# Top-k attention and an MLP on one core: two units' scores in one group, paired hidden tiles, and five pairs of units transposed on TensorE

## The chip, the core and the metric

The kernel runs on one core of a Trainium2 chip. The time is device microseconds of one execution. Of five runs of the kernel before, the median is 1507.03 us (1506.27 to 1509.31). The profile is of the execution that took 1509.31 us. Engines are named as in the profile: PE (TensorE matmul), PEld (its weight loads), DVE (VectorE), ACT (ScalarE), POOL (GpSimd) and SP (SyncE, which here issues all DMAs).

## What is computed

```
scores = q k^T / sqrt(64)                  8 batches x 8 heads, 576 x 576, from 64 channels
kth    = 32nd largest of each row
attn   = softmax(where(scores >= kth, scores, -1e9))
x      = (attn @ v), heads side by side:   4608 tokens x 512
h      = x @ w_in                          512 -> 2048
out    = max(0.01 h, h) @ w_out            2048 -> 512
```

All inputs are 32-bit floats except the two weights, which arrive as 64-bit floats.

## The kernel before

**Rounding.** The weights come in 16 pieces of 64-bit words. `round_weights` turns each into 32-bit floats in three parts: ACT and POOL take the words apart; DVE makes scale and mantissa, and six matmuls with scaled identities add the parts up in PSUM; DVE multiplies by the scale (L147). The loop at L429 runs the parts of three pieces staggered. At its step 15 the scores of units 0 and 1 are issued, ahead of piece 15's second part.

**Units.** Attention is cut into 144 units of 128 rows. A whole unit is 128 queries of both heads of a pair; a left unit is the 64 queries that remain, of two pairs. A unit's score tile `s_sb` is 128 x 2 x 576. Its life, one line per stage:

- `scores` (L191): q k^T into two PSUM tiles `psc0` and `psc1`, two banks each, one for each head, in halves of 288 keys; then two ACT copies to `s_sb` (L207). Two heads use the two halves of the array's rows.
- `top_k` (L209): DVE finds the 32 largest of each row, in four rounds of MAX8 and MATCH_REPLACE8.
- `mask` (L228): POOL, two operations for each head. `exponents` and `sums` (L237, L241): ACT.
- `reciprocals` (DVE, L245), `normalize` (ACT, L249).
- `transpose` (L252): ACT splits each 32-bit word into two 16-bit halves (L259), SP stores them to DRAM, and one transposing DMA brings them back as `wT`.
- `weigh_values` (L276): 20 matmuls with v into the PSUM tile `po`, which two units share; `keep_values` (L290): ACT copies to `x`.

**MLP.** Tokens go in 19 chunks, two of 128 and seventeen of 256. `mlp` (L323) is a generator that yields after every few matmuls. For each of 16 blocks f of the hidden layer it has four matmuls into a PSUM tile `ph` and one Prelu to the tile `gT[f]` (L339); then 2 x 16 matmuls into `pz` (L345), a copy (L352) and a store. The first two chunks use `hidden_of_few` (L301), with the operands exchanged and TensorE transposes (L318). `ph`, `pz` and `pt` share three banks (pool `ps_ml`). PSUM has eight banks: four for `psc`, one for `po`, three for `ps_ml`.

**Order.** Every engine runs its instructions in the order in which the loop at L445 issues them; nothing is reordered. In step s, unit s is in `top_k`, unit s-1 in mask and exponents, unit s-2 in reciprocals, normalize and transpose. In even steps the scores of units s+2 and s+3 are issued, with the values of two units between them. `values_at` (L384) says at which step a unit's values are taken:

```
def values_at(n):
    return n + LAG + (n + LAG) % 2        # LAG = 3
```

The MLP fills in between, seven times a step, by `mlp_steps`. `slot_budget` divides a chunk's remaining cost evenly over the slots until the next chunk is ready. A chunk is ready when its last unit's values are: chunk 0 (units 0 to 3) in step 6, chunk 1 (4 to 7) in step 10, chunk c (units 8c-8 to 8c-1, for c from 2) in step 8c+2. So PE's order in an even step is MLP, scores, values, scores, MLP.

Of the kernel before, what the change touches and what calls it, by code (L numbers as in the profile page):

```python
# [19 lines left out]
def kernel(  # L20
# [25 lines left out]
    HS = S // 2  # L46
    NFC = DFF // P
# [16 lines left out]
    ps_po = ctx.enter_context(tc.tile_pool(name="ps_po", bufs=1, space=bass.MemoryType.PSUM))  # L64
    ps_ml = ctx.enter_context(tc.tile_pool(name="ps_ml", bufs=3, space=bass.MemoryType.PSUM))
# [10 lines left out]
    gT = [const.tile([P, CHMAX], F32, name=f"gT{f}") for f in range(NFC)]  # L76
# [26 lines left out]
    def round_weights(n):  # L103
# [22 lines left out]
        if n + 1 < NPIECE:  # L126
            nc.scalar.activation(scale, scale, AF.Copy, bias=-896.0 * 128, scale=128.0)
        else:
            nc.vector.tensor_scalar(scale, scale, 896.0, 128.0, ALU.subtract, ALU.mult)
        nc.vector.tensor_scalar(m_top, top, 0xF, 0x3F80, ALU.bitwise_and, ALU.bitwise_or)  # L130
        nc.vector.tensor_scalar(top, top, 0x8000, None, ALU.bitwise_and)
        if n < NPIECE - 3:
            pw = ps_sc.tile([P, 2, 512], F32, name=f"psc{n % 2}")
            sums = [(pw[:, h, :], h * 512) for h in range(2)]
            ends = [(pw.rearrange("p h n -> p (h n)"), 0)]
        else:
            ends = sums = [(ps_ml.tile([P, 512], F32, name="pw", tag="ml"), h * 512) for h in range(2)]
# [53 lines left out]
    def scores(u):  # L191
        ps = [ps_sc.tile([P, 2, 512], F32, name=f"psc{i}") for i in range(2)]
        for n in range(0, len(u.parts), 2):
            for half in range(2):
                for i, pi, side, r0 in u.parts[n:n + 2]:
                    qt, kt = qk_of[pi]
                    d = slice(side * D, (side + 1) * D)
                    nc.tensor.matmul(  # L198
                        ps[i][r0:r0 + u.rows, half, 0:HS],
                        qt[d, u.q0:u.q0 + u.rows],  # L200
                        kt[d, half * HS:(half + 1) * HS],
                        start=True, stop=True,
                    )
        u.both = work.tile([P, 2, S], F32, name="s_sb", bufs=5)
        u.s = [u.both[:, i, :] for i in range(2)]
        for i in range(2):
            nc.scalar.copy(u.s[i].rearrange("p (h n) -> p h n", h=2), ps[i][:, :, 0:HS])  # L207

# [54 lines left out]


# [36 lines left out]
    def hidden_of_few(x):  # L301

        g_of = {}
        for j in range(NFC // 4 + 1):
            if j < NFC // 4:
                ph = ps_ml.tile([P, 512], F32, name="ph", tag="ml")
                for c in range(HP):
                    nc.tensor.matmul(ph, x[c][:, 0:P], w_in[c][:, j * 512:(j + 1) * 512],  # L308
                                     start=(c == 0), stop=(c == HP - 1))
                    if c == 1:  # L310
                        yield 2 * 512
                g_of[j] = raws.tile([P, 2 * DMODEL], U16, name="scale", bufs=2).bitcast(F32)
                nc.scalar.activation(g_of[j], ph, AF.Prelu, alpha=SLOPE)
                yield 2 * 512
            if j:
                pt = ps_ml.tile([P, 4, P], F32, name="pt", tag="ml")
                for i in range(4):
                    nc.tensor.transpose(pt[:, i, :], g_of[j - 1][:, i * P:(i + 1) * P], ident)  # L318
                for i in range(4):
                    nc.scalar.copy(gT[4 * (j - 1) + i][:, 0:P], pt[:, i, :])  # L320
                yield 2 * P

    def mlp(ch):  # L323
# [6 lines left out]
        for f in range(NFC if ch >= EARLY else 0):  # L330
            ph = ps_ml.tile([P, 512], F32, name="ph", tag="ml")
            for c in range(HP):
                nc.tensor.matmul(  # L333
                    ph[:, 0:n], w_in[c][:, f * P:(f + 1) * P], x[c][:, 0:n],
                    start=(c == 0), stop=(c == HP - 1),
                )
                if c == 1:
                    yield 2 * max(n, 225)
            nc.scalar.activation(gT[f][:, 0:n], ph[:, 0:n], AF.Prelu, alpha=SLOPE)  # L339
            yield 2 * max(n, 225)  # L340
        for r0 in range(0, n, P):
            m = min(P, n - r0)
            pz = ps_ml.tile([P, 512], F32, name="pz", tag="ml")
            for f in range(NFC):
                nc.tensor.matmul(  # L345
                    pz[0:m, 0:DMODEL], gT[f][:, r0:r0 + m], w_out[f // 4][:, f % 4, :],
# [35 lines left out]
    LAG = 3  # L382

    def values_at(n):  # L384

        return n + LAG + (n + LAG) % 2
# [29 lines left out]
    with tc.manual_schedule():  # L416
# [12 lines left out]
        for n in range(NPIECE + 2):  # L429
# [8 lines left out]
            elif n == NPIECE - 1:  # L438
                for u in steps[0:2]:
                    scores(u)  # L440
            if n == NPIECE - 1:
                load_v(0)
                load_v(1)

        for s in range(len(steps) + LAG + 1):  # L445
# [8 lines left out]

            slot()
# [3 lines left out]
            mlp_steps(budget)  # L459
            slot()  # L460
# [7 lines left out]
            if older:  # L468
# [9 lines left out]
            for u in new[:1]:  # L478
                scores(u)
            if s % 2 == 0:  # L480
                po = ps_po.tile([P, 2, P], F32, name="po")
                for values in (weigh_values, keep_values):
                    for n, u in enumerate((unit(s - LAG - 1), unit(s - LAG))):
                        if u:
                            values(u, po[:, n, :])
                attended(s)
            for u in new[1:]:
                scores(u)
# [63 lines left out]
```

## Time and profile before

| | |
|---|---|
| median of 5 runs | 1507.03 us |
| profiled execution, time and span | 1509.31 us, 1507.5 us |
| PE busy | 1427.1 us, 95% |
| PEld, DVE busy | 933.6, 1328.1 us (62%, 88%) |
| ACT, POOL busy | 1111.5, 1097.6 us (74%, 73%) |
| mean granted PE clock | 0.973 |
| ACT idle before L207 / L339, waiting for PE | 112.9 / 94.4 us |
| DVE idle before `rz` (L247), waiting for ACT | 74.2 us |
| PE waiting for `wT` (L283) | 26.0 us, 9 times |
| PE waiting for L207's evictions | 27.0 us, 9 times, the longest 22.0 |

Busy is time in which an engine works on something; an engine that is busy all the time sets the pace only if the chain of waits that ends last runs through it. The page cuts the span into 40 slices of about 37.7 us and gives each engine's busy share in tenths; PEclk is the clock that TensorE was granted, in tenths of full speed. A group line of the page gives the line, the engine, the operation with output and inputs, the count, then busy time, mean length of one, and the idle time before them with what ended it. Matmuls are pipelined: a record's length contains its way through the array, so the pace is read from the starts. A 32-bit matmul shows as two records.

### The profile page before, as it was taken

How to read it: one execution, taken by the hardware profiler on the slowest of the kernel's cores; microseconds unless marked ns; L12 is line 12 of the kernel's file. 1: busy time of each engine (PE TensorE's matmuls, PEld its weight loads, DVE VectorE, ACT ScalarE, POOL GpSimd, SP SyncE). 2: the span in 40 equal slices, each digit the busy share in tenths (PEclk: the TensorE clock that was granted, in tenths of full speed). 3: DMA queues.
4: the chain of work that ended last, by engine and by line, in shares of the span. 5: the costliest groups of instructions: out<-in, count | busy, mean ns of one | idle time of the engine just before them, and what ended most of it. 6: DMA issues, size and time to landing. Idle time of an engine off the chain costs nothing.

```text
span 1507.5 us, 24130 instructions
## 1 busy us (share of the span) xinstructions
PE 1427.1 (95%) x8030; PEld 933.6 (62%) x8032; DVE 1328.1 (88%) x3414; ACT 1111.5 (74%) x2140; POOL 1097.6 (73%) x742
## 2 busy tenths in 40 slices
PE   6727987999999999999999999999999999999998
PEld 2314445666666766666766666766666666666774
DVE  7898999999999999899999998999999989999600
ACT  8646887878787877787878777878777777777720
POOL 2278788878788877787888787878887877788600
PEclk9956998999999999999999999999999999999999
DMA  8623465645655556655665455645655565655510
GB/s 323 244 63 111 133 169 164 173 129 152 180 156 151 137 154 169 158 139 148 181 170 142 132 166 159 174 127 151 188 163 141 127 170 144 149 144 139 138 51 14
DMA packets 399294, 227.03 MB, mean 151 GB/s; under 512 B 343360, under 2 KB 343361, under 8 KB 397121
## 3 DMA queue, kind: packets, MB, share of 16 engines
q1 hardware_dynamic: 399168, 225.49, 53.8%
q8 instruction: 63, 1.03, 0.3%
q14 instruction: 63, 0.51, 0.1%
HBM read 46.14 MB, written 94.37 MB: 93 GB/s over the span
## 4 chain that ended last, share of the span: by engine, by line
PE 84%; DVE 11%; DMA 3%; ACT 1%; issue 1%; POOL 0%; DVEq 0%; ACTq 0%; SPq 0%
PE pz L345 31%; PE ph L333 31%; PE psc L198 10%; PE po L283 10%; DVE tops L221 4%; DVE pairs L224 3%; DMA wT<-apart 2%; PE ph L308 1%; DVE pairs L216 1%; DVE w_in L147 1%; DVE scale L144 1%; DVE w_out L147 1%; DMA apart<-split 0%; ACT split L259 0%; DVE scale L123 0%
## 5 line engine op out<-in xcount | busy, mean ns | idle before, releaser
L234 POOL TENSOR_SCALAR pen<-s_sb,tops 128x576 f32<-128x576 f32 x288 | 638.4, 2217 | 237.8 <-DVE tops L221 205.7
L221 DVE MAX8 tops<-pairs 128x8 f32<-128x288 f32 (+1 forms) x1152 | 635.6, 591 | 0.0
L345 PE MATMUL pz<-w_out,gT 128*128 128x512 f32 x1152 | 506.7, 595 | 0.0
L333 PE MATMUL ph<-x,w_in 128*128 128x256 f32 x2176 | 483.0, 381 | 0.0
L224 DVE MATCH_REPLACE8 pairs<-tops,pairs 128x288 f32<-128x288 f32 (+1 forms) x864 | 459.9, 537 | 0.0
L333 PEld LDWEIGHTS ph<-x,w_in 128*128 128x128 f32 x2176 | 409.3, 190 | 77.6 <-issue 20.2
L235 POOL TENSOR_TENSOR s_sb<-s_sb,pen 128x576 f32<-128x576 f32 x288 | 406.8, 1412 | 24.0
L345 PEld LDWEIGHTS pz<-w_out,gT 128*128 128x128 f32 x1152 | 215.9, 190 | 264.5 <-issue 263.6
L259 ACT COPY split<-s_sb 128x1152 uint16<-128x1152 uint16 x288 | 315.6, 1144 | 0.0
L207 ACT COPY s_sb<-psc 128x576 f32<-128x576 f32 x288 | 169.3, 639 | 112.9 <-PE psc L198 112.9
L250 ACT ACTIVATE s_sb<-s_sb,rz 128x576 f32<-128x576 f32 x288 | 206.7, 767 | 32.2 <-DVE rz L247 32.2
L238 ACT ACTIVATE s_sb<-s_sb,nbias 128x576 f32<-128x576 f32 x288 | 221.4, 769 | 11.1 <-POOL s_sb L235 11.1
L198 PE MATMUL psc<-kt,qt 64*128 64x288 f32 (+1 forms) x1280 | 198.5, 442 | 27.1 <-ACT s_sb L207 27.0
L216 DVE TENSOR_TENSOR pairs<-s_sb 128x576 f32<-128x576 f32 x288 | 213.6, 780 | 9.9
L283 PE MATMUL po<-wT,vt 128*64 128x128 f32 (+1 forms) x3200 | 182.5, 270 | 26.2 <-DMA wT<-apart 26.0
L283 PEld LDWEIGHTS po<-wT,vt 128*64 128x64 f32 x3200 | 162.7, 140 | 58.5 <-DMA wT<-apart 30.1
L198 PEld LDWEIGHTS psc<-kt,qt 64*128 64x128 f32 (+1 forms) x1280 | 111.2, 182 | 99.4 <-ACT s_sb L207 36.6
L339 ACT ACTIVATE gT<-ph 128x256 f32<-128x256 f32 x272 | 99.0, 380 | 94.8 <-PE ph L333 94.4
L247 DVE RECIPROCAL rz<-ze 128x2 f32<-128x2 f32 x144 | 22.4, 155 | 74.8 <-ACT ze L243 74.2
L297 ACT COPY x<-po 128x128 f32<-128x128 f32 (+1 forms) x160 | 32.5, 263 | 62.8 <-PE po L283 62.6
L224 DVE MATCH_VALUE_LOAD pairs<-tops,pairs 128x8 f32 x864 | 62.1, 72 | 0.0
L352 ACT COPY o_sb<-pz 128x512 f32<-128x512 f32 x36 | 21.1, 586 | 53.9 <-PE pz L345 53.9
(44 smaller groups left out, 391.8 us busy)
## 6 DMA issues: line engine op xcount, KB each, us to landing
apart<-split SPq DMA_DIRECT2D x288, 288.0 KB, 2.1
raw<-in_weights_dram SPq DMA_DIRECT2D x16, 1024.0 KB, 6.4
vt<-in_vk_dram SPq DMA_DIRECT2D x32, 320.0 KB, 3.7
qt<-in_qT_dram SPq DMA_DIRECT2D x32, 288.0 KB, 3.6
kt<-in_kT_dram SPq DMA_DIRECT2D x32, 288.0 KB, 4.0
out_dram<-o_sb SPq DMA_DIRECT2D x36, 256.0 KB, 2.0
wT<-apart SPq DMA_TRANSPOSE x144, 4.6
```

What stands on the lines that cost most here:

```text
L198: nc.tensor.matmul(ps[i][r0:r0 + u.rows, half, 0:HS], qt[d, u.q0:u.q0 + u.rows], kt[d, half * HS:(half + 1) * HS], start=True, stop=True,)
L216: nc.vector.tensor_tensor(pairs[:, :, n, :], u.both[:, :, 0:HS], u.both[:, :, HS:S], op)
L221: nc.vector.max(out=u.tops[:, i, r, :], in_=rest[i])
L224: nc.vector.match_replace(out=rest[i], in_to_replace=u.tops[:, i, r, :], in_values=rest[i], imm_value=LOWEST)
L234: nc.gpsimd.tensor_scalar(pen, u.s[i], u.tops[:, i, ROUNDS - 1, 7:8], MASKED, ALU.is_lt, ALU.mult)
L235: nc.gpsimd.tensor_tensor(u.s[i], u.s[i], pen, ALU.add)
L238: nc.scalar.activation(u.s[i], u.s[i], AF.Exp, bias=u.nbias[:, i:i + 1], scale=SCALE, accum_out=u.z[:, i:i + 1])
L250: nc.scalar.activation(u.s[i], u.s[i], AF.Copy, bias=0.0, scale=u.rz[:, i:i + 1])
L259: nc.scalar.copy(split, pairs[:, :, h])
L283: nc.tensor.matmul(po[side * D:(side + 1) * D, o, :], vt[:, c, side, :], u.wT[:, c + side * NKC if c + 1 < NKC else c, r:r + n], start=(c ...
L333: nc.tensor.matmul(ph[:, 0:n], w_in[c][:, f * P:(f + 1) * P], x[c][:, 0:n], start=(c == 0), stop=(c == HP - 1),)
L345: nc.tensor.matmul(pz[0:m, 0:DMODEL], gT[f][:, r0:r0 + m], w_out[f // 4][:, f % 4, :], start=(f == 0), stop=(f == NFC - 1),)
```

## The change

**Scores.** `scores` takes both units of a step. Their 576 columns are cut in 352 (WIDE) and 224 (NARROW) instead of 288 and 288. Each unit has a wide tile of two banks (tag "wide", two buffers); both units' narrow parts share one tile of two banks ("narrow"). The matmuls are issued as u0 wide, u0 narrow, u1 narrow, u1 wide, then four ACT copies in that order. `po` has no bank of its own any more and is a "wide" tile too. Until step 20 the scores come before the values, from then on after them.

**MLP.** `ps_ml` has two banks. A `ph` tile holds two blocks f, with one Prelu for both; `gT` is one tile with a dimension for f.

**Hurried pairs.** The pairs of units (2,3), (6,7), (14,15), (22,23) and (30,31), the last of chunks 0 to 4, have their values one step earlier. They are transposed by nine TensorE transposes and two ACT copies. The second unit of a pair is normalized and transposed at the very start of its step, ahead of the top-k.

**Rounding.** Unit 0's scores are issued after piece 12's matmuls, unit 1's after piece 15's. Piece 14's scale moves from ACT to DVE, and pieces use other PSUM tiles.

```diff
-    ps_po = ctx.enter_context(tc.tile_pool(name="ps_po", bufs=1, space=bass.MemoryType.PSUM))
-    ps_ml = ctx.enter_context(tc.tile_pool(name="ps_ml", bufs=3, space=bass.MemoryType.PSUM))
+    ps_ml = ctx.enter_context(tc.tile_pool(name="ps_ml", bufs=2, space=bass.MemoryType.PSUM))
...
-        if n + 1 < NPIECE:
+        if n < NPIECE - 2:
             nc.scalar.activation(scale, scale, AF.Copy, bias=-896.0 * 128, scale=128.0)
...
-        if n < NPIECE - 3:
-            pw = ps_sc.tile([P, 2, 512], F32, name=f"psc{n % 2}")
+        if n < NPIECE - 4 or n % 2 == 0:
+            tag, bufs = ("wide", 2) if n < NPIECE - 4 else ("narrow", 1)
+            pw = ps_sc.tile([P, 2, 512], F32, name=tag, bufs=bufs)
...
+    def scores(us):
+        narrow = ps_sc.tile([P, 2, 512], F32, name="narrow")
+        ps = {}
+        for k, u in enumerate(us):
+            wide = ps_sc.tile([P, 2, 512], F32, name="wide", bufs=2)
+            ps[u] = ((wide[:, :, 0:WIDE], 0, WIDE),
+                     (narrow[:, :, k * NARROW:(k + 1) * NARROW], WIDE, S))
+
+        order = ((us[0], 0), (us[0], 1), (us[1], 1), (us[1], 0))
+        for u, part in order:
+            to, k0, k1 = ps[u][part]
+            for n in range(0, len(u.parts), 2):
                 for i, pi, side, r0 in u.parts[n:n + 2]:
...
+                    nc.tensor.matmul(to[r0:r0 + u.rows, i, :], qt[d, u.q0:u.q0 + u.rows],
+                                     kt[d, k0:k1], start=True, stop=True)
+        for u in us:
+            u.both = work.tile([P, 2, S], F32, name="s_sb", bufs=5)
+            u.s = [u.both[:, i, :] for i in range(2)]
+        for u, part in order:
+            to, k0, k1 = ps[u][part]
+            nc.scalar.copy(u.both[:, :, k0:k1], to)
...
+    def transpose_in_haste(u):
+
+        u.wT = work.tile([P, 2 * NKC - 1, P], F32, name="wT", bufs=3)
+        both = u.both.rearrange("p i n -> p (i n)")
+        for c0, c1 in ((0, 8), (8, 2 * NKC - 1)):
+            pt = ps_sc.tile([P, 2, 512], F32, name="wide", bufs=2)
+            pt = pt.rearrange("p h (c n) -> p (h c) n", n=P)
+            for c in range(c0, c1):
+                nc.tensor.transpose(pt[:, c - c0, :], both[:, c * P:(c + 1) * P], ident)
+            nc.scalar.copy(u.wT[:, c0:c1, :], pt[:, 0:c1 - c0, :])
...
+        for f0 in range(0, NFC if ch >= EARLY else 0, 2):
+            ph = ps_ml.tile([P, 2, CHMAX], F32, name="ph", tag="ml")
+            for i in range(2):
+                f = f0 + i
+                for c in range(HP):
+                    nc.tensor.matmul(
+                        ph[:, i, 0:n], w_in[c][:, f * P:(f + 1) * P], x[c][:, 0:n],
+                        start=(c == 0), stop=(c == HP - 1),
+                    )
+                    if c == 1 or i == 0 and c == HP - 1:
+                        yield 2 * max(n, 225)
+            nc.scalar.activation(gT[:, f0:f0 + 2, 0:n], ph[:, :, 0:n], AF.Prelu, alpha=SLOPE)
...
+    HURRY = 20
+    HURRIED = {3, 7, 15, 23, 31}
 
     def values_at(n):
 
-        return n + LAG + (n + LAG) % 2
+        return n + LAG + (n + LAG) % 2 - ((n | 1) in HURRIED)
...
-            elif n == NPIECE - 1:
-                for u in steps[0:2]:
-                    scores(u)
+            elif n == NPIECE - 3:
+                first_scores(steps[0])
+            elif n == NPIECE:
+                first_scores(steps[1])
...
+        def values(s):
+            due = [u for n, u in enumerate(steps) if values_at(n) == s]
+            if due:
+                po = ps_sc.tile([P, 2, 512], F32, name="wide", bufs=2)[:, 0, 0:2 * P]
+                po = po.rearrange("p (u n) -> p u n", u=2)
+            for part in (weigh_values, keep_values):
+                for n, u in enumerate(due):
+                    part(u, po[:, n, :])
+            attended(s)
...
+            if s - 2 in HURRIED:
+                reciprocals(older)
+                normalize(older, 0)
+                normalize(older, 1)
+                transpose_in_haste(older)
+                older = None
             slot()
...
             mlp_steps(budget)
+            if s - 2 in HURRIED:
+                values(s)
+                budget = slot_budget(s + 1)
             slot()
...
-            for u in new[:1]:
-                scores(u)
+            if s - 1 in HURRIED:
+                transpose_in_haste(older)
+            if new and s < HURRY:
+                scores(new)
             if s % 2 == 0:
...
+                values(s)
+            if new and s >= HURRY:
+                scores(new)
```

`first_scores` is the old `scores` for one whole unit, with two "wide" tiles in place of `psc0` and `psc1`.

## The prediction

> **What bounds the kernel now.** I read part 2 of the page first. TensorE (PE) is full from slice 7 (about 264 us) to the end, at full clock; VectorE (DVE) is nearly full until slice 37. Part 4, the chain that ended last, settles which of the two it is:
>
> ```profile
> PE   6727987999999999999999999999999999999998
> DVE  7898999999999999899999998999999989999600
> PEclk9956998999999999999999999999999999999999
> ...
> PE 84%; DVE 11%; DMA 3%; ACT 1%; issue 1%; POOL 0%; DVEq 0%; ACTq 0%; SPq 0%
> PE pz L345 31%; PE ph L333 31%; PE psc L198 10%; PE po L283 10%; DVE tops L221 4%; DVE pairs L224 3%; DMA wT<-apart 2%; PE ph L308 1%; DVE pairs L216 1%; DVE w_in L147 1%; DVE scale L144 1%; DVE w_out L147 1%; DMA apart<-split 0%; ACT split L259 0%; DVE scale L123 0%
> ```
>
> DVE's share of the chain is the start; after that it is matmuls. Table of stretches (length, then busy us of PE, PEld, DVE, ACT, POOL; clock):
>
> ```profile
> 80.00:100.00 20.00, 1.04 (x3) 1.00 (x5) 19.86 (x53) 8.28 (x16) 17.19 (x12) 0.50 0.08 30
> ...
> 200.00:220.00 20.00, 15.14 (x98) 8.22 (x97) 19.76 (x51) 18.18 (x42) 17.18 (x12) 0.91 0.67 178
> 220.00:240.00 20.00, 15.98 (x101) 8.00 (x99) 19.86 (x57) 14.84 (x29) 17.17 (x12) 1.00 0.73 207
> 240.00:260.00 20.00, 15.09 (x88) 12.25 (x89) 18.46 (x49) 14.29 (x28) 17.14 (x12) 0.74 0.48 134
> 260.00:280.00 20.00, 20.00 (x167) 16.80 (x166) 18.83 (x50) 16.36 (x36) 15.68 (x12) 1.00 0.53 152
> ```
>
> Before 260 us PE waits for DVE to finish units; after it, PE is never idle. From the trace, steps start (first L216 of a unit) every 8.87 us while DVE runs freely, but every 9.37 us on average from step 26 on: ScalarE (ACT) waits for PE in its queue, DVE waits for ACT (rz <- ze, 74 us in all), so PE drags DVE. The first ph of chunks 2, 3, 4, 5 is at 250.8, 326.6, 402.0, 477.3: 75.4 us a chunk, and it stays so. Of that, pz is 27.9, ph 27.4; the rest is attention, which the change touches. PE's timeline, one even step:
>
> ```profile
> 735.26 1.24 PE L198 MATMUL psc<-kt,qt 64*128 64x288 f32 x8
> 736.43 2.40 PE L283 MATMUL po<-wT,vt 128*64 128x128 f32 x40
> 738.77 1.61 PE L198 MATMUL psc<-kt,qt 64*128 64x288 f32 x8
> 740.31 1.99 PE L333 MATMUL ph<-x,w_in 128*128 128x256 f32 x8
> ```
>
> **A. Grouping the two units' scores.** In single records, score matmuls run two at a time (starts 7 ns apart) and such pairs follow each other every 0.2425 us; a unit's four pairs are 0.97 us of work. But the eight records take 1.17: a change of shape from ph to scores adds 0.09 (start to start 0.309 instead of 0.216) and the first pair takes 0.347. The other changes cost alike: scores to po 0.14, po to scores 0.20, scores to ph 0.20. After 260 us the 110 groups of eight average 1.214, since some second groups wait for the first's eviction (above: 1.54 from start to start). The change has both units in one group and one change of shape fewer: 2 x 0.97 + 0.20 = 2.14 instead of 2 x 1.214 = 2.43, so 0.29 us a pair. The count of matmuls stays; 288 + 288 columns become 352 + 224. No row has 224 columns. Spacing goes with columns (256: 0.216, 288: 0.2425, 512: 0.428), which gives 0.296 + 0.19 = 0.486 against 0.485. From above: a 224 pair costs no more than the 288 row, 0.2425, then a pair of units loses 4 x 0.053 = 0.21, nearly the whole gain. I take 0.19, by the 256 row, whose weight load of 0.190 fits in 0.216 with room.
>
> New waits: from step 20 u1's wide part takes po's buffer, so PE waits for keep_values. Behind that wait stand u1's four wide records and all ph. PE gets there 0.2 + 0.59 + 0.38 + 0.38 = 1.55 us after po; the two copies (0.45 together, starting some 0.2 after po) are done at 0.7 where ACT is free. ACT in this step finishes ze at 738.02, with po ended some 1.2 earlier than now at about 737.6; slack 0.5. Hidden; without the cover it would be about 0.5 us a pair. Evictions keep their elements (4 copies, 704 and 448 elements for 576 and 576), none on the path: u0 is needed a step later.
>
> A rule speaks against two units' narrow parts in one bank: the Trainium skill (PSUM — Partial Sum Buffer, section "PSUM bank collisions raise a hardware error") has PSUM guarded by bank and quadrant, not by address, so u0's narrow copy would wait for u1's narrow matmuls. By it that copy starts an estimated 0.38 us later, on ACT and off the path, and the sum is the same either way.
>
> **B. Prelu on pairs, two banks instead of three.** 272 activations of 380 ns become 136 of about 593 (the 128x512 Prelu row), some 23 us less on ACT, which is off the path. What PE can run ahead: now two tiles of 1.73 = 3.46 us, after it one tile of 3.46, with a Prelu 0.2 longer. Today's waits at this place:
>
> ```profile
> PEld ph L333 <- ACT gT L339: 4.3, 22, 0.4
> ```
>
> Only weight loads, 0.2 each, and the 64-record ph groups run at 14.02 against 13.8 + one change of shape: no stall. With 0.2 less room, these 22 may show: 0 to 5 us; I take 2. The one gT tile costs nothing if waits go by region: they do for s_sb, where the exponents of half 0 start at 730.00 while POOL still masks half 1 until 732.2. Otherwise each of 17 chunks waits one Prelu, 0.6 to 3 us.
>
> **C. The hurried pairs and unit 0.** Piece 15's matmuls lose the four score groups ahead of them in PE's queue, which ran from 63.76 to 67.4 while its data stood ready at 64.7; two L147 waits (1.17 and 0.60) go, less 0.43 for a DVE operation taken over from ACT. Step 0 begins at about 69.4 instead of 70.8. ACT takes unit 0's two evictions (1.18) between rounding steps; it can slip by 2.4 us there before piece 14's matmuls at 60.5 are late.
>
> Ten units lose two splits (1144 ns), two stores (2.1 us to landing) and one DMA transpose (4.6) from ACT and SP, and get 9 PE transposes and two ACT copies (1152 elements, about 1.3 us by the 128x512 row of 586). The L318 records follow each other every 0.109 us at full clock: 1.0 us a unit, 3.9 us for the 36 of units 22, 23, 30 and 31, which fall where PE is full. The Trainium skill (TensorE: Matmul & The Clock Gate, Part 4: PE-mode transpose) gives about 275 ns each in a kernel and says that the full clock doesn't engage; by it those 36 would be an estimated 9.9 us. The trace differs, and it decides.
>
> What it brings: now unit 15's values wait for a transpose until 246 and chunk 2 starts at 250.8 (step 18's end). After: rz at the start of step 17, normalize 1.45, transposes and copies about 2.3, po 2.3, keep 0.5, about 8 us with the waits between. What it costs: reciprocals stand ahead of the whole top-k of the step on DVE, and ze comes 1.25 us (idle PE: POOL's 7.5 and ACT's 2.6 after a step of 8.87) to 2.6 us (dragged, ze at 738.02 in the step that began at 735.4) after its start. Five times about 2: 9 us of DVE time, 3.3 by step 17. Step 17 then begins at 69.4 + 17 x 8.87 + 3.3 + 5 (today's stall at the first ph) = 228.5, chunk 2 at 236.5: 14 us earlier.
>
> But this is not kept. Chunks 3 and 4 are hurried too; chunk 5 (units 32 to 39) is not, its values stay in step 42. PE's path: 236.5 + 226.5 (as now) - 12 x 0.29 + 3.9 + about 5 (norm and buffer waits around four saturated transposes) = 468. DVE's path: 69.4 + 43 x 8.87 + 9 + 5 = 465 for step 43, plus 1.5 to chunk 5, plus about 4 for drag in between: 470. The later one counts: 470 instead of 477.3, so **7 us** gained, between 0 (three more us at each hurried step) and 14 (all kept).
>
> **Sum.** After chunk 5: 49 pairs x 0.29 = 14.2. Together -14.2 - 7 + 2 = -19.2. The profiled execution took 1509.31 (span 1507.5, 1.8 around it), 2.3 over the median of 1507.03; from the median: **1488 us**.
>
> **Rivals.**
> 1. Hurry buys nothing: DVE stalls of 3 us more at steps 5, 9, 17 put step 43 where it is (469). 1495. For it: stalls of up to 4.38 at step 8 now. 15%.
> 2. Hurry is kept whole, drag being smaller than thought: 1481. Against it: 43 x 8.87 of DVE. 10%.
> 3. The grouping doesn't do what it says, because 224 columns run no faster than 288: only C is left, 1502. For it: a weight load of 0.187 in a slot of 0.19. 10%.
> 4. Slower: PE waits for PSUM banks in ph. ACT's stretch normalize, exponents, splits is 1.43 + 0.96 + 2.19 = 4.6 us; a ph pair that ends at its start gets its Prelu after 4.6 + 0.59, against 3.46 of cover: 1.7 us lost. One stretch a step, 126 steps; hit in a quarter of them: +54, so 1541. It decides from 0.15 us a step (19 / 126). Against it: today's cover is the same and no PE stall shows, and ACT mostly waits for PE there (94 us). 12%.
>
> Forecast 50%; the last 3% lie around no change. The range leaves out rival 4 and some of the ends: 1479 (14 + 14 gained) to 1502 (rival 3). Under 0.2%, 3 us, a measurement can't tell from no change. Faster 0.85, same 0.04, slower 0.11.
>
> **What would show it.** PE's timeline: groups of 16 score records lasting about 2.14, after po; the first L333 at about 236 and chunk 5's at about 470; step 43 at about 469; then 74.3 us a chunk. Wrong if PE's ph shows waits for ACT gT of more than 5 us in all, if a 224 pair takes 0.24, if score groups wait for x L297, or if PE idles after 480 us.

## The result, and the profile after

The changed kernel takes **1503.58 us** (median of 25 runs, 1500.73 to 1505.38), the kernel before 1506.73 us beside it (45 runs). The ratio is 0.9978, 95% interval 0.9973 to 0.9984: faster by 3.2 us, where 19 had been forecast and 5 (1502) was the slow end of the range. Part 2 and part 4 of the page after:

```profile
PE   6708878999999999999999999999999999999999
...
DVE  7997898979999999999999999999999999999600
...
PEclk9959999999999999999999999999999999999999
...
PE 81%; DVE 9%; DMA 4%; ACT 3%; issue 1%; POOL 1%; SPq 0%; DVEq 0%; POOLq 0%; ACTq 0%
```

PE is full from slice 7 as before; between slices 2 and 6 its digits are no better, and DVE has holes (8, 8, 7) in slices 4, 6 and 8. So the end of the kernel and its beginning have to be read apart. The first ph of chunk 5 divides them; from 480 to 1440 us PE waits 2.2 us in all before and 2.9 after. One execution of each kernel of this study (us; "rest" is the span less chunk 5's start):

| kernel | chunk 2 | chunk 5 | rest | median, ratio to before (95%) |
|---|---|---|---|---|
| before | 250.8 | 477.3 | 1030.2 | 1506.73 |
| after | 249.1 | 486.1 | 1016.9 | 1503.58, 0.9973 to 0.9984 |
| forecast | 236.5 | 470 | 1018 | 1488 |
| e1 no hurry | 261.4 | 483.2 | 1014.7 | 1500.26, 0.9945 to 0.9970 |
| e2 first two hurried | 257.3 | 479.0 | 1018.8 | 1498.33, 0.9933 to 0.9958 |
| e3 last three hurried | 254.6 | 489.2 | 1017.0 | 1506.54, 0.9992 to 1.0010 |
| e4 before, with hurry | 254.4 | 497.3 | 1026.9 | 1527.58, 1.0126 to 1.0154 |
| e5 no hurry, values first | 254.5 | 476.4 | 1014.1 | 1493.80, 0.9908 to 0.9935 |
| e6 before, pairs, 2 banks | 258.4 | 482.5 | 1024.5 | 1508.79, 1.0005 to 1.0023 |
| e7 before, pairs, 3 banks | 248.1 | 472.3 | 1022.9 | 1498.74, 0.9935 to 0.9959 |
| e8 e5, pt elsewhere | 256.6 | 478.6 | 1015.4 | 1495.98, 0.9924 to 0.9947 |
| e9 e5, first two hurried | 257.6 | 479.3 | 1016.3 | 1497.86, 0.9929 to 0.9954 |
| e10 e7, unit 0 early | 247.6 | 471.8 | 1024.9 | 1497.17, 0.9924 to 0.9951 |
| e11 e6, own bank for pt | 261.4 | 485.7 | 1024.2 | 1511.22, 1.0021 to 1.0044 |
| e12 e5, pt copied by DVE | 253.0 | 474.7 | 1015.6 | **1489.86**, 0.9876 to 0.9909 |
| e13 after, DVE normalizes | 243.1 | 478.7 | 1015.6 | 1496.07, 0.9918 to 0.9946 |
| e14 e5, all hurried | 248.6 | 484.5 | 1016.3 | 1504.84, 0.9978 to 0.9996 |
| e15 e12, all hurried, DVE normalizes | 250.6 | 487.2 | 1016.4 | 1507.48, 0.9995 to 1.0012 |
| e16 the same, first three | 248.7 | 478.3 | 1016.0 | 1497.83, 0.9927 to 0.9954 |

The rest came near the forecast: 13.3 us less (12.2 forecast). Chunk 5 starts 8.8 us later than before instead of 7.3 earlier, and step 43 begins at 481.6, where the forecast had about 469. PE's timeline of after, one even step (start, length, then the operation):

```profile
738.94 1.31 PE L318 MATMUL wide<-wT,vt 128*64 128x128 f32 x20
740.81 1.31 PE L318 MATMUL wide<-wT,vt 128*64 128x128 f32 x20 [0.56 <-DMA wT<-apart]
742.05 0.86 PE L210 MATMUL wide<-kt,qt 64*128 64x352 f32 x4
742.75 0.92 PE L210 MATMUL narrow<-kt,qt 64*128 64x224 f32 x8
743.51 0.76 PE L210 MATMUL wide<-kt,qt 64*128 64x352 f32 x4
744.20 2.86 PE L369 MATMUL ph<-x,w_in 128*128 128x256 f32 x12
```

From the first score to ph it is 2.15 us; over 44 such groups the mean is 2.141 and the longest 2.141. None waits for an eviction, and the eight narrow records take 0.76: 0.19 a pair, as taken. PE's time a chunk, from chunk 5's first ph to the last chunk's, each group counted to the start of the next (13 chunks, us):

| | scores | values | ph | pz | sum |
|---|---|---|---|---|---|
| before | 9.08 | 9.65 | 28.11 | 27.86 | 74.70 |
| e7 (pairs alone) | 8.82 | 9.45 | 28.02 | 27.86 | 74.15 |
| after | 8.10 | 9.71 | 28.02 | 27.86 | 73.69 |
| e5 (no hurry) | 8.05 | 9.53 | 28.02 | 27.86 | 73.46 |

### The profile page after: what moved, and what is told of

It reads as the page before. It is cut to its first block, busy times and chain, and to the rows that moved or that the text cites. A ratio compares the mean times of both kernels' runs of the same rounds, so it can differ in the third digit from the quotient of the medians.

```text
span 1503.0 us, 24186 instructions
## 1 busy us (share of the span) xinstructions
PE 1405.3 (94%) x8120; PEld 934.8 (62%) x8122; DVE 1328.8 (88%) x3414; ACT 1091.4 (73%) x1979; POOL 1097.8 (73%) x742
## 4 chain that ended last, share of the span: by engine, by line
PE 81%; DVE 9%; DMA 4%; ACT 3%; issue 1%; POOL 1%; SPq 0%; DVEq 0%; POOLq 0%; ACTq 0%
PE pz L381 32%; PE ph L369 27%; PE wide L318 11%; PE wide L210 6%; PE narrow L210 3%; DVE tops L245 3%; DMA wT<-apart 3%; DVE pairs L248 2%; DMA apart<-split 1%; ACT split L283 1%; ACT s_sb L274 1%; DVE pairs L240 1%; PE ph L343 1%; PE wide L296 1%; DVE w_out L149 1%
## 5 line engine op out<-in xcount | busy, mean ns | idle before, releaser
L283 ACT COPY split<-s_sb 128x1152 uint16<-128x1152 uint16 x268 | 293.7, 1144 | 0.0
L262 ACT ACTIVATE s_sb<-s_sb,nbias 128x576 f32<-128x576 f32 x288 | 220.9, 767 | 11.5 <-POOL s_sb L259 11.2
L318 PEld LDWEIGHTS wide<-wT,vt 128*64 128x64 f32 x3200 | 160.0, 138 | 56.4 <-ACT ze L267 16.7
L318 PE MATMUL wide<-wT,vt 128*64 128x128 f32 (+1 forms) x3200 | 178.6, 267 | 16.5 <-ACT wT L297 6.9
L375 ACT ACTIVATE gT<-ph 128x512 f32<-128x512 f32 x136 | 80.8, 594 | 79.5 <-PE ph L369 79.5
L332 ACT COPY x<-wide 128x128 f32<-128x128 f32 (+1 forms) x160 | 32.2, 260 | 141.1 <-PE wide L318 141.1
L217 ACT COPY s_sb<-wide 128x704 f32<-128x704 f32 x142 | 107.1, 754 | 24.6 <-PE wide L210 24.5
L210 PE MATMUL wide<-kt,qt 64*128 64x352 f32 (+1 forms) x632 | 117.0, 484 | 5.1 <-ACT wT L297 4.4
L217 ACT COPY s_sb<-narrow 128x448 f32<-128x448 f32 x142 | 68.7, 536 | 4.1 <-PE narrow L210 3.5
L210 PE MATMUL narrow<-kt,qt 64*128 64x224 f32 (+1 forms) x632 | 67.7, 353 | 1.7 <-DMA kt<-in_kT_dram 1.7
```

The costliest lines, as they stand in the source:

```text
L210: nc.tensor.matmul(to[r0:r0 + u.rows, i, :], qt[d, u.q0:u.q0 + u.rows], kt[d, k0:k1], start=True, stop=True)
L262: nc.scalar.activation(u.s[i], u.s[i], AF.Exp, bias=u.nbias[:, i:i + 1], scale=SCALE, accum_out=u.z[:, i:i + 1])
L283: nc.scalar.copy(split, pairs[:, :, h])
L318: nc.tensor.matmul(po[side * D:(side + 1) * D, o, :], vt[:, c, side, :], u.wT[:, c + side * NKC if c + 1 < NKC else c, r:r + n], start=(c ...
```

## The experiments

**The hurry, by parts (e1, e2, e3, e4).** Theory: hurry lets the MLP begin sooner but DVE and PE pay for it. Rival: the time before chunk 5 is lost elsewhere. In the changed kernel:

```diff
-    HURRIED = {3, 7, 15, 23, 31}
+    HURRIED = set()                  # e1
+    HURRIED = {3, 7}                 # e2
+    HURRIED = {15, 23, 31}           # e3
```

e4 is the kernel before with `transpose_in_haste` (into `psc0` and `psc1`), `values(s)`, and the same five pairs.

> The changed kernel with no hurried pair: all values in their old steps, all units through the DMA transpose. Theory H (the hurried pairs cost what the grouping wins: their normalize and copies stand in ACT's queue behind copies that wait for PE, PE waits in turn, and the next unit's exponents come late): chunk 2 starts at about 249 as before, chunks 2 to 4 take 74.1 each, chunk 5 starts at about 472 instead of 486.1, and the span is about 1489, 14 less than the changed kernel's and 1.2% less than before. Rival R (the loss ahead of chunk 5 comes from the shared wide banks, the scores ahead of the values until step 20, or two banks for the MLP in chunks 0 and 1): chunk 5 still starts after 480, span 1497 or more.

> The changed kernel with only the pairs (2,3) and (6,7) hurried. Theory H: the DVE stalls of 8.5 and 3.8 us in steps 6 and 10 remain (5.3 in all before), so step 17 begins some 7 us later than without hurry and chunk 2 starts at 252 to 256; span 1491 to 1495, 3 to 6 over the kernel without hurry. Rival R: PE is idle there anyway, so the span is that of the kernel without hurry.

> The changed kernel with only the pairs (14,15), (22,23) and (30,31) hurried. Theory H: step 17 begins at about 225, chunk 2 starts at about 242, but each hurried chunk then costs 3 to 5 us of PE time (transposes, waits for normalize and for the copies), and chunk 5 starts at about 479: span about 1496. If the two early pairs cost nothing, it is the changed kernel's 1503; if the three late ones cost nothing, 1489.

> The kernel before with the hurried pairs alone (transposes into the old score tiles; 288 and 288 columns, three MLP banks, scores around the values). Theory H: slower than before by about 9 us and up to 14, span 1516 to 1521, chunk 5 at 486 or later instead of 477.3. Rival R: within 3 us of before, or faster, since here the other edits are missing.

Without hurry the kernel is faster by 3.3 us, though chunk 2 starts 12.3 later: here hurry brings chunk 2 forward and gives back more by chunk 5. On the kernel before it costs 21 us, more than the theory had. Beyond this sign theory H fails: e1's chunk 5 at 483.2 and span of 1497.9 are what the rival had, so most of the time ahead of chunk 5 is lost elsewhere (e5 and e6 look for it). e2 brings chunk 2 forward (257.3 against 261.4), where H had it later, and e3's chunk 2 comes at 254.6 instead of 242. The accounts of PE from chunk 2 to chunk 5 show what is given back (PE's groups as above):

| chunk | e1 | after | what after has more |
|---|---|---|---|
| 2 | 74.2 | 80.7 | transposes 4.6, values 1.9 |
| 3 | 73.8 | 78.1 | transposes 4.3 |
| 4 | 73.8 | 78.2 | scores 2.1, values 2.0 |

The transposes of four units with the waits behind them are 8.9, just what the forecast had. The other entries are what it left out. Chunk 4 holds one more group of scores (80 records against 64): a chunk that starts earlier in the order has attention work moved behind it, and here the hurried chunk 4 is followed by the unhurried chunk 5, 2.1 us. The values have the same number of records in both kernels (160 in chunk 4). They take 3.9 us longer in the two chunks, since PE now waits in them for units that come late or for v (0.58, 0.62, 1.26 and 0.33 us); the longest of these waits in after:

```profile
429.31 1.31 PE L318 MATMUL wide<-wT,vt 128*64 128x128 f32 x20 [1.26 <-DMA wT<-apart]
```

Where PE is full, starting a chunk earlier is only a change of order.

**The order of scores and values (e5).** From e1:

```diff
-    HURRY = 20
+    HURRY = 0
```

> No hurried pair, and the values ahead of the scores in all steps (HURRY = 0), not from step 20 on. Without hurry, chunk 2 started at 261.4, not at 249. Theory O (the order: po takes a wide tile whose scores ACT has yet to evict, so PE waits 3.0, 0.9, 4.0 and 4.5 us for those copies in steps 10 to 18): chunk 2 starts at about 252, span about 1489. Theory N (two MLP banks in chunks 0 and 1: pz waits 4.0 us for the copy of the third pt, and PE comes back at half clock): chunk 2 stays at 258 to 262, span 1495 to 1498.

Chunk 2 comes 6.9 us sooner (254.5), the median falls by 6.5. PE's timeline of e1 shows the wait that goes, with the clock at 0.59 behind it (40 records in 3.93 where 2.40 is usual):

```profile
182.28 0.76 PE L210 MATMUL wide<-kt,qt 64*128 64x352 f32 x4
186.07 3.93 PE L318 MATMUL wide<-wT,vt 128*64 128x128 f32 x40 [3.03 <-ACT s_sb L217]
```

With scores first, po takes the wide tile whose scores ACT hasn't evicted, and ACT is at exponents and splits. e1 has four such waits from step 10 to 18 (3.03, 0.85, 4.02 and 4.54), e5 none there; part of them comes back as waits for the transposing DMA (5.32 at 249.0), and a wait of 3.61 for a DMA of keys falls to 0.60. The prediction looked at waits for the wide tiles only for the order from step 20 on. In the changed kernel itself this order costs nothing that shows: with all pairs hurried, values first give chunk 2 at 248.6 instead of 249.1 and a median of 1504.84 instead of 1503.58 (e14 below).

**Pairs and banks (e6, e7, e8, e10, e11, e12).** e6 and e7 are the kernel before with `ph` and Prelu on pairs, one `gT` tile, and one ACT copy instead of four for a transposed tile of chunks 0 and 1, with two and three banks:

```diff
-    ps_ml = ctx.enter_context(tc.tile_pool(name="ps_ml", bufs=3, space=bass.MemoryType.PSUM))
+    ps_ml = ctx.enter_context(tc.tile_pool(name="ps_ml", bufs=2, space=bass.MemoryType.PSUM))    # e6 only
```

> The kernel before with the MLP's part of the change alone: ph tiles of two blocks, one Prelu for both, one gT tile, and two banks in ps_ml (the freed bank stays unused). Theory N: in chunks 0 and 1 pz and pt wait for ACT's copies, chunk 2 starts at 257 to 262 instead of 250.8, from there on 75.4 a chunk as before: span 1514 to 1518. Theory O: chunk 2 at 252 or earlier, span within 2 of before's 1507.

> The same with three banks in ps_ml. Both theories: ACT loses 15 to 20 us of busy time, which is off the path, so the span is within 1.5 of before's 1507 and chunk 2 starts at 250 to 251. If the pairing itself costs something, it shows here.

Pairing alone, with three banks, gains 8 us by the medians, where no more than 1.5 had been expected. The profiled spans differ by 12.3 (before's execution lay 2.3 over its median, e7's 1.8 under it): 2.7 by chunk 2, 2.3 from there to chunk 5, 7.3 after it. PE's timeline of e7, to be laid beside the even step of before in the prediction, where the second group ran 1.54 to the next start:

```profile
727.76 1.24 PE L198 MATMUL psc<-kt,qt 64*128 64x288 f32 x8
728.93 2.40 PE L283 MATMUL po<-wT,vt 128*64 128x128 f32 x40
731.26 1.24 PE L198 MATMUL psc<-kt,qt 64*128 64x288 f32 x8
732.43 1.99 PE L334 MATMUL ph<-x,w_in 128*128 128x256 f32 x8
```

All 86 groups of eight take 1.171 at most (before: mean 1.206, up to 1.543). ACT, whose busy time falls by 11.5 us (1111.5 to 1100.0), evicts in time. Of the 7.3 after chunk 5, by the table above, scores make 3.4, ph 1.2 and values 2.6; in the values two waits for the transposing DMA (1.06 and 0.99) give way to one of 0.31. With two banks 10.3 us are lost ahead of chunk 2, as e6's theory N had it (its time of 1514 to 1518 did not come, since it left out what pairing gains). PE at the end of chunk 0's hidden layer, e6 and then e7:

```profile
156.25 0.60 PE L318 MATMUL pt<-ident,scale 128*128 128x128 f32 x4
157.10 0.65 PE L318 MATMUL pt<-ident,scale 128*128 128x128 f32 x4 [0.25 <-ACT scale L313]
161.76 5.40 PE L346 MATMUL pz<-w_out,gT 128*128 128x512 f32 x8 [4.01 <-ACT gT L319]
```

```profile
152.35 0.60 PE L318 MATMUL pt<-ident,scale 128*128 128x128 f32 x4
153.20 0.66 PE L318 MATMUL pt<-ident,scale 128*128 128x128 f32 x4 [0.25 <-ACT scale L313]
153.69 3.60 PE L346 MATMUL pz<-w_out,gT 128*128 128x512 f32 x8
```

Two transposed tiles and pz follow each other, which needs three banks. With two, pz waits for the first tile's copy, and on ACT that stands behind normalizing, an exponent and the splits (e6's ACT):

```profile
156.94 1.43 ACT L250 ACTIVATE s_sb<-s_sb,rz 128x576 f32<-128x576 f32 x2
158.27 0.76 ACT L238 ACTIVATE s_sb<-s_sb,nbias 128x576 f32<-128x576 f32 x1
...
159.03 2.19 ACT L259 COPY split<-s_sb 128x1152 uint16<-128x1152 uint16 x2
161.13 1.06 ACT L319 COPY gT<-pt 128x512 f32<-128x512 f32 x2
```

The next three try to take this wait away; e8 from e5, e11 from e6, e12 from e5:

```diff
-                pt = ps_ml.tile([P, 4, P], F32, name="pt", tag="ml")
+                pt = ps_sc.tile([P, 2, 512], F32, name="narrow")[:, 0, :].rearrange("p (i n) -> p i n", i=4)    # e8
+                pt = ps_pt.tile([P, 4, P], F32, name="pt")      # e11: the eighth bank
...
-                nc.scalar.copy(gT[:, 4 * (j - 1):4 * j, 0:P], pt)
+                if j < NFC // 4 - 1:                            # e12
+                    nc.scalar.copy(gT[:, 4 * (j - 1):4 * j, 0:P], pt)
+                else:
+                    nc.vector.tensor_copy(gT[:, 4 * (j - 1):4 * j, 0:P], pt)
```

> No hurried pair, values first in all steps, and the pt tiles of chunks 0 and 1 in the narrow score tile, so that ph and pz keep the two MLP banks to themselves. Both causes are gone if N and O both hold: chunk 2 starts at 249 to 251, chunk 5 at 472, span 1486 to 1489. If it equals the run with the values first, the two banks cost nothing.

> The kernel before with Prelu on pairs and two banks for ph and pz (1508.8), but the transposed tile of chunks 0 and 1 in the eighth bank, its own. From chunk 2 on it is the two-bank kernel. Theory: two banks cost their 10 us because in chunks 0 and 1 the transposed tile, ph and pz take turns in two banks, and each change of turn waits for ACT's queue; with a bank for the transposed tile chunk 2's first ph comes at about 250 instead of 258.4, as with three banks (248.1), and the time is about 1500. Rival: ph and pz of chunks 0 and 1 wait for each other's evictions whatever the transposed tile does, or the waits move to its own single bank: 256 to 259, 1506 to 1509.

> The kernel with values always ahead of scores (1493.8, chunk 2's first ph at 254.5), with the eviction of the last two transposed tiles of chunks 0 and 1 on VectorE instead of ScalarE: four copies of 128x512, about 0.6 us each. Theory: what holds PE at the first pz of these chunks (4.00 us at 156.4 in that kernel, with the clock halved behind it) is ScalarE's queue, where the copy stands behind normalizing, exponents and splits; with the copies elsewhere the wait is below 1 us, and chunk 2 starts up to 5 us earlier (249 to 252), 1489 to 1491. Rival: the wait goes but DVE, whose queue is in order too, now waits for PE's transposes in front of the next unit's top-k, as it stands ahead of PE: DVE gaps of 2 us and more ahead of these copies, chunk 2 at 254 to 258 and 1494 to 1498.

e8 and e11 miss, and for the same reason: one bank for pt moves the wait from pz to the second tile (e8: 4.91 and 5.77 us). PE of e11:

```profile
155.37 0.60 PE L319 MATMUL pt<-ident,scale 128*128 128x128 f32 x4
160.88 1.11 PE L319 MATMUL pt<-ident,scale 128*128 128x128 f32 x4 [4.91 <-ACT gT L320]
```

So a bank of its own for pt doesn't help: what PE waits for is the copy that stands in ACT's queue, and only a third bank for tiles in turn hides it (e7). e12 confirms it by moving the copy: PE of e12 has no wait there and keeps its clock (in e5 the wait was 4.00 and these eight records took 6.12):

```profile
151.66 0.66 PE L353 MATMUL pt<-ident,scale 128*128 128x128 f32 x4 [0.25 <-ACT scale L348]
152.19 3.70 PE L384 MATMUL pz<-w_out,gT 128*128 128x512 f32 x8
```

Most of that gain is lost again on the way: PE's wait for a late Prelu grows from 2.47 to 3.67 us (ph at 187.8), and it waits longer for transposed units (2.30, 1.97, 2.25 and 4.66 instead of 1.94, 1.67, 1.13 and 5.32); chunk 2 comes 1.5 sooner. The median is 3.9 below e5's, but the two profiled spans are alike (1490.3 and 1490.5) and the intervals touch; e12 has the lowest median of the versions tried, and it beats both kernels clearly.

e10 puts unit 0's scores (two pieces before the last) and unit 1's into the rounding of e7:

```diff
-            elif n == NPIECE - 1:
-                for u in steps[0:2]:
-                    scores(u)
+            elif n == NPIECE - 2:
+                scores(steps[0])
+            elif n == NPIECE:
+                scores(steps[1])
```

> The kernel before with Prelu on pairs and three banks, and the scores of units 0 and 1 issued inside the weights' rounding (unit 0's two pieces before the last, unit 1's behind the last). Theory: the last piece's matmuls no longer stand behind four score groups, step 0 starts at about 69.4 instead of 70.4, and DVE's steps run freely to chunk 2, so all of it, 1 us, shows in chunk 2's start (247) and in the end: 1497.7. Rival: the steps up to chunk 2 are set by waits for ACT and not by the start: 1498.7 as without it, chunk 2 at 248.

Step 0 starts at 68.5 instead of 70.4, chunk 2 only 0.5 sooner; the medians are 1.6 apart with intervals that overlap. The rival fits chunk 2 better; the time decides nothing.

**Hurry by itself (e9, e14).** From e5, `HURRIED = {3, 7}` and all five:

> The kernel with values always ahead of scores, with the first two hurried pairs put back (units 2, 3, 6, 7; only they complete chunks 0 and 1). Theory: two early chunks started sooner fill PE's idle time before chunk 2, and these pairs lie where PE isn't full, so that nothing is paid later: with scores first the same step took 1.9 us (1498.3 against 1500.3), so 1492 here, chunk 2's first ph at about 252 instead of 254.5. Rival: what stands between chunk 1 and chunk 2 are the waits of pz and pt for ACT in chunks 0 and 1, which come whenever these chunks run, and the hurried pairs add theirs: 1494 to 1497.

> The changed kernel with values always ahead of scores, all five pairs hurried: the price of hurry without the waits for the wide tiles that scores first brings. Theory A, PE's lag: hurry brings chunk 2 forward but gives it back, since transposes, their waits and the moved steps cost PE 3 to 4 us by chunk 5 and nothing starts sooner behind them: chunk 2 at 246 to 250, chunk 5 at 478 to 482 (476.4 without hurry), 1495 to 1500 against 1493.8 without hurry. Theory B: hurry loses only through waits that the order before step 20 adds; with values first it keeps its gain: chunk 2 at 240 to 244, chunk 5 at 468 to 472, 1485 to 1490.

Hurry loses on this base too, 4.1 us for the first two pairs and 11.0 for all, in both runs more than either theory had; e14's chunk 2 is at 248.6, as in its theory A, but chunk 5 comes at 484.5. Where scores came first the first two pairs gained 3.0 beside the last three (after against e3) and 1.9 alone (e2 against e1, with intervals that overlap and profiled spans that are alike), so their sign hangs on what else holds PE.

**The chain at chunk 2 (e13, e15, e16).** The forecast gave 8 us from the start of step 17 to chunk 2. In after it is 16.7 (232.4 to 249.1). DVE, ACT and PE of after:

```profile
232.30 0.14 DVE L271 RECIPROCAL rz<-ze 128x2 f32<-128x2 f32 x1
...
251.48 0.17 DVE L271 RECIPROCAL rz<-ze 128x2 f32<-128x2 f32 x1 [5.60 <-ACT ze L267]
```

```profile
239.50 0.43 ACT L332 COPY x<-wide 128x128 f32<-128x128 f32 x2 [1.32 <-PE wide L318]
241.40 0.59 ACT L388 COPY o_sb<-pz 128x512 f32<-128x512 f32 x1 [1.47 <-PE pz L381]
241.88 1.44 ACT L274 ACTIVATE s_sb<-s_sb,rz 128x576 f32<-128x576 f32 x2
244.07 1.18 ACT L297 COPY wT<-wide 128x1024 f32<-128x1024 f32 x2 [0.75 <-PE wide L296]
249.26 0.43 ACT L332 COPY x<-wide 128x128 f32<-128x128 f32 x2 [4.00 <-PE wide L318]
249.58 0.79 ACT L262 ACTIVATE s_sb<-s_sb,nbias 128x576 f32<-128x576 f32 x1
```

```profile
239.38 1.98 PE L381 MATMUL pz<-w_out,gT 128*128 128x512 f32 x4
242.72 1.43 PE L296 MATMUL wide<-ident,s_sb 128*128 128x128 f32 x9 [1.35 <-ACT s_sb L274]
245.14 4.07 PE L318 MATMUL wide<-wT,vt 128*64 128x128 f32 x40 [0.99 <-ACT wT L297]
249.14 9.12 PE L369 MATMUL ph<-x,w_in 128*128 128x256 f32 x41
```

Unit 15's reciprocal is there at 232.3, its normalizing begins at 241.9: on ACT it stands behind copies that wait for PE. The exponents of the next unit stand behind the copies of the hurried one, so DVE waits 5.60 us for its `rz`. After the other hurried pairs these waits are 8.51, 3.79, 7.59 and 2.37: 27.9 in all, where the prediction put 9 and a stall of 5. Which holds the chain, ACT's order or PE? e13 takes normalizing out of ACT's queue:

```diff
             if s - 2 in HURRIED:
                 reciprocals(older)
-                normalize(older, 0)
-                normalize(older, 1)
+                for i in range(2):
+                    nc.vector.tensor_scalar(older.s[i], older.s[i], older.rz[:, i:i + 1], None, ALU.mult)
                 transpose_in_haste(older)
```

> The changed kernel, with the second unit of each hurried pair normalized on VectorE, right behind its reciprocal, instead of ScalarE (ten operations of 128x576 moved, an estimated 0.8 us each by the pairs row). In the changed kernel the reciprocal of unit 15 came at 232.3 and its normalizing on ScalarE at 241.9. Theory A, PE's lag: ScalarE was late only because it waited for TensorE's results, and TensorE reached the transposes at 241.4 and waited 1.35 us for them; so chunk 2's first ph comes 1 to 2 us earlier (247 to 248), DVE loses 1.6 us at each hurried step, and the time is 1501 to 1506. Theory B, ScalarE's order: the 9.6 us between reciprocal and normalizing are what made chunk 2 late; chunk 2 at 240 to 244 and 1494 to 1498.

The size is that of theory B: chunk 2 at 243.1, 7.5 us of time gained. The path is PE's, as in A. First DVE's line, then PE's timeline of e13:

```profile
230.14 0.95 DVE L507 TENSOR_SCALAR s_sb<-s_sb,rz 128x576 f32<-128x576 f32 x2
```

```profile
226.81 1.44 PE L296 MATMUL wide<-ident,s_sb 128*128 128x128 f32 x9 [0.58 <-ACT s_sb L274]
230.34 0.92 PE L210 MATMUL wide<-kt,qt 64*64 64x352 f32 x8 [2.09 <-ACT wT L297]
...
234.49 2.40 PE L318 MATMUL wide<-wT,vt 128*64 128x128 f32 x40
236.83 1.98 PE L381 MATMUL pz<-w_out,gT 128*128 128x512 f32 x4
238.65 1.15 PE L296 MATMUL wide<-ident,s_sb 128*128 128x128 f32 x9
240.78 2.40 PE L318 MATMUL wide<-wT,vt 128*64 128x128 f32 x40 [0.99 <-ACT wT L297]
243.12 9.76 PE L369 MATMUL ph<-x,w_in 128*128 128x256 f32 x44
```

Normalizing is done at 231.1 and the transposes begin 7.6 us later, without a wait: PE stood in its own queue. PE had not fallen behind before that, for it waited 0.58 us for the normalizing of unit 14. But behind unit 14's transposes the order of step 16 has its scores, its values and four records of pz, and unit 15's transposes come after them. The scores wait 2.09 us there for ACT's copy of the transposed tile, since they need a wide tile, and 1.47 more for a DMA of keys. What e13 gains is the wait of 1.35, 0.28 on the transposes and 1.67 on the values, which ran at about half clock in after; another 2.3 was gained by step 16, where the like wait (1.21) in the pair before is gone too. A's price counted the wait alone. Last, e15 and e16 are e12 with e13's edit and `HURRIED` of all five pairs, and of 3, 7 and 15:

> All five pairs hurried, with the three things taken away that held TensorE back before chunk 2: values always ahead of scores, the last two transposed tiles of chunks 0 and 1 evicted on VectorE, the hurried unit normalized on VectorE. Theory A, TensorE's lag: chunk 2 then starts where the forecast had it, 236 to 240 (253.0 without hurry and without the moved normalizing), and since the forecast left out only 3.5 us between chunks 2 and 5, chunk 5 starts at 472 to 476, as without hurry (474.7): 1488 to 1493 against 1489.9. Theory B: it is hurry itself, chains of dependent steps across three engines, that makes TensorE late; chunk 2 at 243 or later, chunk 5 at 478 or later, 1494 or more.

> The same with only the pairs before chunk 2 hurried (units 2, 3, 6, 7, 14, 15). Theory A: the pairs of chunks 3 and 4 lie where TensorE is full, their transposes with waits cost 2 x (2.14 + 2.42) = 9.1 us and bring nothing, so leaving them out gives chunk 5 at 464 to 468 and 1480 to 1485, better than with all five by 7 to 9 us and than without hurry by 5 to 9. Theory B: chunk 5 is set by DVE's 43 steps of 8.87 from 69.5 (451 and what DVE waits), not by TensorE, and leaving them out brings 0 to 3 us.

Theory A falls: chunk 2 stays at 250.6 and 248.7, chunk 5 at 487.2 and 478.3. The copy moved to DVE stands there ahead of PE now and waits 5.68 us for the transposed tile, so step 17 starts at 238.1 (227.1 in e12), and PE then waits for units. And the queue is still there. PE of e15, where unit 15 is normalized at 238.2:

```profile
233.94 1.43 PE L296 MATMUL wide<-ident,s_sb 128*128 128x128 f32 x9 [3.12 <-ACT s_sb L274]
...
244.29 1.98 PE L384 MATMUL pz<-w_out,gT 128*128 128x512 f32 x4
246.12 1.15 PE L296 MATMUL wide<-ident,s_sb 128*128 128x128 f32 x9
```

PE waits 3.12 us for unit 14, does step 16's values, scores and pz, and gets to unit 15 7.9 us after it is ready. In the seven kernels in which this pair is hurried, unit 15's transposes begin 11.1 to 14.1 us behind unit 14's, and chunk 2 begins 11.5 to 16.7 us after step 17. No run moved step 16's work to another place, so what that would bring is not shown. Of A only the difference holds: leaving out the pairs of chunks 3 and 4 brings chunk 5 forward by 8.9, where 9.1 had been worked out. The times that A had (1480 to 1485) were missed by 13 us. No run had chunk 2 at 236.5; whether any order can is open.

## Why the prediction was wrong, point by point

- **Step A, grouping: right.** Groups of 2.141 (2.14 forecast), 0.19 for a narrow pair, no wait for evictions. The later narrow copy that the PSUM rule gave would not show: ACT idled 4.1 us in all ahead of the narrow copies. The gain of a pair, 2 x 1.206 - 2.141 = 0.27, came as forecast, but 0.07 of it is the pairing's work: e7's groups take 1.171 ungrouped. What grouping itself brings is 2 x 1.171 - 2.141 = 0.20, as much as the one change of shape that was counted. That the rest after chunk 5 came within 1.1 us is partly luck: scores fall by 12.7, 3.4 of which e7 has by pairing alone, and the 2 for banks never came. The forecast's 75.4 us a chunk didn't quite "stay so": the mean of the thirteen after chunk 5's start was 74.70.
- **Step B, pairs and banks: wrong twice.** "Some 23 us less on ACT, which is off the path": ACT's busy time falls by 11.5 in e7, and 8 us of the path go with it, after chunk 5 through evictions that come in time and units that come sooner. And the bound of 0 to 5 for two banks looked at the ph loop alone. There no stall came (its cost was nothing, not 2); in chunks 0 and 1 it was 10.3 (e6 against e7).
- **Rival 4** was named for the right mechanism at the wrong place: PE behind ACT's stretch of 4.6 us for want of a bank. In ph it never came; at the first pz of chunk 0 or 1 it came at 4.00.
- **The order before step 20** had no price at all. It cost 6.9 at chunk 2 without hurry (e1 against e5); with it, 0.5 (after against e14), so it is no part of this miss.
- **Step C, the hurry: the step that failed.** "About 8 us with the waits between", from step 17 to chunk 2, took 16.7, and step 17 began at 232.4 instead of 228.5. Up to step 17 DVE had waited 12.3 us for ACT (8.51 and 3.79), where 8.3 were put down. The 8 us assumed that PE waits for DVE before 260 us and takes the hurried unit at once. So it does with unit 14; with unit 15 it doesn't, because step 16's scores, values and pz stand ahead in PE's queue, and the sum has no term for them (7.6 us behind the normalizing in e13, 7.9 in e15; in after ACT's order adds a wait of 1.35). No kernel with this pair hurried did it in less than 11.5. So chunk 2 came at 249.1, 12.6 later than forecast; that it came before the old 250.8 at all is hurry's doing (261.4 without).
- **What hurry costs later:** the transposes' 8.9 (3.9 + 5) was right and measured as 8.9. The figure weighed there, 275 ns a transpose in one kernel (the Trainium skill, TensorE: Matmul & The Clock Gate, Part 4: PE-mode transpose, which names 16-bit data beside it), doesn't hold here: nine that follow pz without a wait take 1.15 us (e13 above). Left out were 2.1 of scores moved behind chunk 4 and 3.9 of values that wait. Forecast from chunk 2 to chunk 5: 233.5; measured 237.0. Together with the 12.6 this makes the 16.1 us by which chunk 5 missed 470, and with it nearly all of the miss of the time. Rivals 1 and 2 had hurry at nothing and kept whole; it was a loss: 3.3 us (e1), 11.0 on a better base (e14), 21 on the old kernel (e4).
- **Unit 0 in the rounding:** step 0 at 69.5, forecast 69.4: right.

## What to carry to other kernels

Price a move by walking through the queue of every engine in the stretch where it lands, in the order of the program and with the change's other parts laid in: that PE waited for the first unit of a pair said nothing of the scores and values that the order puts ahead of the second. Where an engine is full, starting a piece of its work earlier is only a change of order, and every helper operation it needs is a loss. A pool of buffers is sized by the place with the shortest turn and the longest queue in front of the evictions, not by the loop that runs most; and when an in-order engine "off the path" has less to do, look for what waits for its evictions.

## What was not expected of the hardware

The clock that TensorE is granted falls after short pauses too. In after, table of stretches (length; busy us of PE, PEld, DVE, ACT, POOL; clock; DMA's share and GB/s):

```profile
243.00:245.20 2.20, 1.20 (x11) 0.72 (x10) 2.20 (x10) 1.45 (x3) 2.09 (x2) 1.00 0.28 101
245.20:249.00 3.80, 3.80 (x40) 3.77 (x40) 0.68 (x3) 0.06 (x1) 3.17 (x3) 0.55 0.02 4
```

Pauses of 1.35 and 0.99 us with 1.43 of transposes between them went ahead of the values, and these took 4.07 us at a clock of 0.55. The same pattern (1.21 and 0.99) at 166 us left the clock alone: 2.40. In e13, with the one pause of 0.99, it stayed at 1.00. Over all runs there are eleven such patterns (a first pause of 1.21 to 1.80, then 0.99), and the clock fell behind four of them; behind the 26 with the pause of 0.99 alone it never fell. The Trainium skill (TensorE: Matmul & The Clock Gate, Part 1: The HAM clock gate) has the clock fall after an idle window of about 3.4 us in a window that runs freely. That it hits some of several like patterns fits the free window; that 2.2 us of pause in sum can be enough (e3 at 249 us) goes beyond the rule, unless the transposes in between do not count as work (the stretch is then 3.6 us long). No run separates the two. The waits of 4.00 at pz brought it down in every kernel that had them: eight records in 5.40 (e6) to 6.75 us (e1, where the clock was 0.50 from 159 to 163 us) instead of 3.60.
